# Two pairs per output group and 512-token feed-forward products in a fused SSD and bilinear FFN kernel

## The chip, the cores and the metric

The kernel runs on one core of a Trainium2 chip. The time is the device time of one execution in microseconds (us). The engines are named as in the profile: PE is TensorE, DVE is VectorE, ACT is ScalarE, POOL is GpSimd, and SP is SyncE, which here only issues DMAs.

## The reference

The input has 4 batches, 8 heads, 768 tokens, a head dimension of 32 and a state dimension of 16. A scan with decay runs along the tokens, then a feed-forward layer of 3072 tokens, 256 model and 1536 inner dimensions follows.

```python
log_a = np.log(np.clip(a, 1e-06, 1.0))
for c in range(nc):
    ...
    L = np.exp(cum[:, :, :, None] - cum[:, :, None, :]) * causal
    M = np.einsum('bhin,bhjn->bhij', Cc, Bc) * L
    y_intra = np.einsum('bhij,bhjd->bhid', M, xc)
    y_inter = np.einsum('bhin,bhnd->bhid', Cc, state) * decay_to_i[:, :, :, None]
    y[:, :, sl] = y_intra + y_inter
    Bx = np.einsum('bhjn,bhjd->bhjnd', Bc, xc) * decay_from_j[:, :, :, None, None]
    state = decay_full[:, :, None, None] * state + np.sum(Bx, axis=2)
...
x = attn_out.transpose(0, 2, 1, 3).reshape(B * S, H * D)
out = ((x @ w_a) * (x @ w_b)) @ w_out
```

## The kernel before

The tokens are cut into 6 blocks of 128. The four batches form two groups of two, so there are 12 pairs: pair p is block p // 2 and batches 2(p % 2) and 2(p % 2) + 1, which makes 256 tokens. One pair passes through these steps.

- Loads (`load1`, L126): B, C and x of a pair, two DMAs each, into buffers bn, cn and xn that exist three times. In the loop all of them go through SP's queue.
- Scaling on POOL: `scale_bc` (L251, L259) multiplies B and C by decay factors (fB, fC, which `fb` at L567 fills per block on DVE), `scale_x` (L245) makes x 16-bit. From pair 4 on, B is also copied into "planes" (L269), and `turn` (L308) lets SP issue a transposing DMA that makes the operands of the scores.
- Scores (L320): 32 small matmuls into four PSUM banks, SC0 and SC1 of two banks each. `mask` (L354) multiplies each bank by the causal mask on DVE and writes 16-bit T1; with `by_pool` ACT copies the bank first (L351) and POOL multiplies (L352).
- The output group: `outputs` (for pairs below 4, `pv`) puts into the same banks the state's part (L425, operand Sbd), the masked scores times x (`pv_u`, L363) and the sums of the next state (`ds_mm`, L380). ACT copies the outputs to X2T (L441 in three pieces). Then `state_sums` adds to the state on DVE (L468), and `state_spread` on POOL makes the next pair's Sbd and gU (L484, L491).
- The feed-forward product: one `unit(p, k2)` computes two of the 12 slices of the inner dimension for 256 tokens. `unit_mm` (L504) makes aps and bps, each four matmuls of 256 columns into one PSUM bank; ACT copies aps to asb (L518); DVE multiplies bps and asb to hk (L525). The four remaining PSUM banks (pool psf) go round among aps, bps and the output product ops in the order of allocation.
- The output product: `out_half` (L538) sums 12 matmuls of 256 columns over hk and Wo for 128 tokens, ACT scales (L553), SP stores (L555).

The order of the work is written out by hand (`manual_schedule`), and each engine takes its instructions in the order of the code. `unit` returns a function: PE's matmuls and ACT's copy stand where `unit` is called, DVE's product stands where the function is called. So masks and products can be put in any order on DVE. A prologue with warm-up matmuls covers pairs 0 to 2; a loop over p from 3 to 11 puts the scores and the group of pair p between the six units of pair p - 1 and the two output products of pair p - 2; a tail finishes pair 11.

In the loop before, the order on PE from pair 4 on is: scores, units 0 to 2, one output product, unit 3, the group, one output product, units 4 and 5. On DVE it is mask 0, product 0, masks 1 and 2, product 1, mask 3, products 2 and 3, the state sums, products 4 and 5.

Of the kernel before, what the change touches and what calls it, by code (L numbers as in the profile page):

```python
# [9 lines left out]
f32 = mybir.dt.float32  # L10
f16 = mybir.dt.float16
# [7 lines left out]
YS = 16.0  # L19
# [3 lines left out]
def kernel(  # L23
# [60 lines left out]
    X2T = big.tile([128, NP, 2, 2, Q], f16, name="X2T")  # L84
# [17 lines left out]
    mid = ctx.enter_context(tc.tile_pool(name="mid", bufs=3))  # L102
    ffh = ctx.enter_context(tc.tile_pool(name="ffh", bufs=4))
    ps4 = ctx.enter_context(tc.tile_pool(name="ps4", bufs=1, space=PSUM))
# [25 lines left out]

    def load(p, eng=None):
        tiles(p)
        return [load1(eng or nc.sync, p, w, bt) for w in range(3) for bt in range(2)]
# [284 lines left out]
    def outputs(p):  # L418
        s = st[p]
        SCt = (SC0, SC1)  # L420
        for m in range(4):
            for bt in range(2):
                rows = slice(32 * m, 32 * m + 32)
                half = 64 * ((m + bt) % 2)
                nc.tensor.matmul(  # L425
                    SCt[bt][half : half + 64, m // 2, 0:Q],
                    s["Sbd"][rows, bt],
                    s["CT"][rows, bt],
                    start=True,
                    stop=False,  # L430
                    skip_group_check=True,
                    tile_position=(32 * m, half),
                )
        py = {(bt, u): SCt[bt][:, u, 0:Q] for bt in range(2) for u in range(2)}
        for u in range(2):
            pv_u(p, u, py, False)
        if p // NBP < NBLK - 1:
            ds_mm(p, 256, [SC0[:, 1], SC1[:, 1]])
        whole, low, high = slice(0, 128), slice(0, 64), slice(64, 128)
        for bt, to, fr in ((0, whole, whole), (1, low, high), (1, high, low)):  # L440
            nc.scalar.activation(  # L441
                out=X2T[to, p, bt].rearrange("p u (i r) -> p u r i", r=2),
                in_=SCt[bt][fr, :, 0:Q].rearrange("p u (r i) -> p u r i", r=2),
                func=AF.Copy,
                scale=YS / XS,
            )
# [115 lines left out]

    def bank(name):
        return psf.tile([128, 512], f32, name=name, tag="ff")
# [81 lines left out]
    load_wo(1)  # L646
    x2 = [load1(nc.sync, 2, 2, bt) for bt in range(2)]
# [26 lines left out]
    load(3)  # L674
# [12 lines left out]
    load(4)  # L687
# [16 lines left out]
    for p in range(3, NP):  # L704
        scores(p)
        ri = p >= P0
        if p + 1 < NP:
            scale_bc(p + 1, 1, nc.gpsimd)
            scale_bc(p + 1, 0, nc.gpsimd)
            turn(p + 1)  # L710
        if (p - 1) // NBP < NBLK - 1:
            state_spread(p - 1)
        if p + 1 < NP:
            scale_x(p + 1, nc.gpsimd)
        if p + 2 < NP:
            load(p + 2)
        if p == 3:
            mask(product(p, 0))
            h()
            for m in range(1, 4):  # L720
                mask(product(p, m))
            out_half(1, 0)
            out_half(1, 1)
            go((2, 2))
        else:
            h = unit(p - 1, 0)
            mask(product(p, 0), ri=ri)
            h()
            mask(product(p, 1), ri=ri)
            mask(product(p, 2), ri=ri)  # L730
            h = unit(p - 1, 1)
            h()
            mask(product(p, 3), ri=ri)
            go((p - 1, 2))
            out_half(p - 2, 0)
            go((p - 1, 3))
        pull(p)
        outputs(p) if ri else pv(p)
        if p // NBP < NBLK - 1:
            state_sums(p)  # L740
        if p == 3:
            go((2, 3))
        else:
            out_half(p - 2, 1)
        if p % 2 == 0 and p // 2 + 1 < NBLK:
            fb(p // 2 + 1)
        go((p - 1, 4), (p - 1, 5))

    go((NP - 1, 0), (NP - 1, 1))
    out_half(NP - 2, 0)  # L750
    go((NP - 1, 2), (NP - 1, 3))
    out_half(NP - 2, 1)
    go((NP - 1, 4), (NP - 1, 5))
    out_half(NP - 1, 0)
    for part in range(2):
        o_ps = bank("ops")
        cols = slice(part * 128, part * 128 + 128)
        for k in range(NK):
            nc.tensor.matmul(  # L759
                o_ps[:, 0:128],  # L760
                st[NP - 1]["hk"][:, k, Q : 2 * Q],
                Wo[:, k, cols],
                start=(k == 0),
                stop=(k == NK - 1),
                skip_group_check=True,
            )
        o_sb = ffh.tile([128, d_model], f32, name="osb", tag="osb")
        if part == 0:
            nc.vector.tensor_scalar(o_sb[:, 0:128], o_ps[:, 0:128], 1.0 / (YS * YS), None, ALU.mult)
        else:  # L770
            nc.scalar.activation(out=o_sb[:, 0:128], in_=o_ps[:, 0:128], func=AF.Copy, scale=1.0 / (YS * YS))
        r0 = (2 * (NBP - 1) + 1) * S + (NBLK - 1) * Q
# [31 lines left out]
```

## Time and profile before

| Quantity | Value |
| --- | --- |
| Median of 3 runs | 127.15 us (127.08 to 128.66) |
| Profiled execution, its own time | 127.25 us |
| Its span, first to last instruction | 125.5 us |
| Granted TensorE clock | 1.000 |
| Busy: PE, DVE, ACT, POOL | 119.9, 88.8, 72.5, 56.6 us |
| PE weight loads (PEld), beside PE | 101.3 us |
| DMA | 13.79 MB, mean 110 GB/s |

The page shows one execution. Busy time is the sum of an engine's instructions. Matmuls are pipelined, so the time between the starts of two matmuls says more than the length of one. The chain of waits follows what ended last back through what released it; its pieces, in order of time, show where PE runs without a hole. In lines of groups, the numbers after the bar are the busy time in us, the mean in ns of one instruction, and the engine's idle time just before, with what ended it. In lines of the timeline, the first number is the start and the second the length, both in us. In lines of DMA issues, the last number is the median time in us from issue to landing.

### The profile page before, as it was taken

Reading aid. Unit: us, or ns where it says so; the run is one execution under the profiler, and the core shown is the slowest. Engines: PE = TensorE matmul, PEld = TensorE weight load, DVE = VectorE, ACT = ScalarE, POOL = GpSimd, SP = SyncE. Lnnn points to the kernel's source line nnn. Section 1 sums busy time; section 2 is a strip of 40 time slices with the busy share of each in tenths; the row PEclk is TensorE's granted clock in tenths of the full one; section 3 lists DMA queues with packets and bytes.
Section 4 is the critical chain, followed back from the end, with each engine's and each line's share of the span. In section 5 each row is a group of like instructions: output and inputs, shape, how many; then the busy total and the mean of one; then the engine's idle time right before and its main releaser. Section 6 shows DMA issues by size and latency. Waiting matters only on the chain.

```text
span 125.5 us, 4786 instructions
## 1 busy us (share of the span) xinstructions
PE 119.9 (96%) x1964; PEld 101.3 (81%) x1964; DVE 88.8 (71%) x165; ACT 72.5 (58%) x144; POOL 56.6 (45%) x100
## 2 busy tenths in 40 slices
PE   6979999999999999999999999999999999999990
PEld 2436789978898988888898898889889889899980
DVE  1588978894958958948959949959849739644440
ACT  0466666866365575575575475485485575674430
POOL 7999974957850933806508307508218000000000
PEclk9999999999999999999999999999999999999999
DMA  3999999974644666547646764454646210110112
GB/s 65 167 167 232 157 213 159 184 145 80 167 89 67 165 115 125 141 71 185 81 74 169 87 107 128 88 108 126 114 82 168 66 42 5 42 42 5 44 45 78
DMA packets 45493, 13.79 MB, mean 110 GB/s; under 512 B 40496, under 2 KB 45264, under 8 KB 45472
## 3 DMA queue, kind: packets, MB, share of 16 engines
q1 hardware_dynamic: 41520, 10.06, 38.4%
q0 software_dynamic: 1952, 3.08, 14.6%
q10 hardware_dynamic: 2000, 0.36, 1.6%
q8 instruction: 15, 0.25, 0.9%
q14 instruction: 6, 0.05, 0.1%
HBM read 11.13 MB, written 3.15 MB: 114 GB/s over the span
## 4 chain that ended last, share of the span: by engine, by line
PE 84%; DMA 6%; POOL 4%; DVE 2%; ACT 1%; issue 1%; ACTq 0%; POOLq 0%
PE aps L504 25%; PE bps L504 24%; PE ops L538 23%; DMA Wb<-in_moe_w_b_dram 6%; PE SC L320 3%; PE SC L363 3%; DVE t L354 2%; PE SC L380 1%; PE SC L425 1%; PE fps L221 1%; POOL cn L126 1%; PE ops L759 1%; POOL bn L126 1%; ACT bt L297 1%; POOL causal L181 1%
## 5 line engine op out<-in xcount | busy, mean ns | idle before, releaser
L525 DVE TENSOR_TENSOR hk<-bps,asb 128x512 f16<-128x512 f32 x72 | 49.1, 686 | 17.8 <-ACT asb L518 17.4
L518 ACT COPY asb<-aps 128x512 f32<-128x512 f32 x72 | 42.0, 586 | 17.4 <-PE aps L504 16.3
L504 PE MATMUL aps<-X2T,Wa 128*128 128x256 f16 x288 | 43.3, 273 | 0.0
L504 PE MATMUL bps<-X2T,Wb 128*128 128x256 f16 x288 | 42.9, 273 | 0.2 <-DMA Wb<-in_moe_w_b_dram 0.2
L538 PE MATMUL ops<-Wo,hk 128*128 128x256 f16 x276 | 33.9, 273 | 0.0
L504 PEld LDWEIGHTS <-Wb 128*128 128x128 f16 x288 | 29.6, 103 | 2.2 <-DMA Wb<-in_moe_w_b_dram 0.4
L504 PEld LDWEIGHTS <-Wa 128*128 128x128 f16 x288 | 28.5, 103 | 3.0 <-DMA Wa<-in_moe_w_a_dram 0.3
L538 PEld LDWEIGHTS <-hk 128*128 128x128 f16 x276 | 26.0, 98 | 3.6 <-DVE hk L525 0.2
L354 DVE TENSOR_TENSOR t<-SC,causal_ri 128x512 f16<-128x512 f32 x32 | 21.1, 680 | 0.0
L251 POOL TENSOR_TENSOR planes<-cn,fC 128x256 f16<-128x256 f32 x8 | 5.0, 621 | 33.7 <-DMA cn<-in_C_dram 23.1
L553 ACT ACTIVATE osb<-ops 128x256 f32<-128x256 f32 x23 | 8.8, 383 | 16.4 <-PE ops L538 16.2
L245 POOL TENSOR_SCALAR x<-xn 128x512 f16<-128x512 f32 x9 | 13.4, 1490 | 1.0 <-DMA xn<-in_x_dram 0.3
L441 ACT ACTIVATE X2T<-SC 64x256 f16<-64x256 f32 (+1 forms) x24 | 10.9, 456 | 4.9 <-PE SC L380 3.8
L468 DVE SCALAR_TENSOR_TENSOR U<-SC,G,gU 128x64 f32<-128x64 f32 x16 | 4.3, 282 | 7.0 <-ACT X2T L441 6.3
L354 DVE TENSOR_TENSOR t<-SC,causal 128x512 f16<-128x512 f32 x13 | 8.3, 682 | 0.9 <-PE SC L320 0.9
L259 POOL TENSOR_TENSOR bm<-bn,fB 128x256 f16<-128x256 f32 x11 | 7.0, 640 | 1.5 <-DMA bn<-in_B_dram 1.5
L193 PE MATMUL SC<-warm 128*128 128x512 f16 (+1 forms) x15 | 4.9, 474 | 1.2 <-DVE warm L162 1.2
L193 PEld LDWEIGHTS <-warm 128*128 128x128 f16 x22 | 2.3, 122 | 3.7 <-issue 1.9
L363 PEld LDWEIGHTS <-x 64*32 64x32 f16 x384 | 3.2, 91 | 2.2 <-ACT x L243 1.0
L363 PE MATMUL SC<-t,x 64*32 64x128 f16 x352 | 4.6, 219 | 0.0
L269 POOL COPY planes<-bm 128x128 f16<-128x128 f16 x16 | 4.2, 291 | 0.5
L352 POOL TENSOR_TENSOR t<-tmp,causal 128x512 f16<-128x512 f32 x3 | 3.5, 1156 | 1.3 <-DMA cn<-in_C_dram 1.0
(78 smaller groups left out, 81.0 us busy)
## 6 DMA issues: line engine op xcount, KB each, us to landing
out_dram<-osb SPq DMA_DIRECT2D x23, 128.0 KB, 2.5
xn<-in_x_dram SPq DMA_DIRECT2D x21, 128.0 KB, 3.8
bn<-in_B_dram SPq DMA_DIRECT2D x20, 64.0 KB, 3.0
cn<-in_C_dram SPq DMA_DIRECT2D x18, 64.0 KB, 3.1
Wa<-in_moe_w_a_dram POOLq DMA_DIRECT2D x2, 384.0 KB, 6.1
Wb<-in_moe_w_b_dram POOLq DMA_DIRECT2D x2, 384.0 KB, 7.5
Wo<-in_moe_w_out_dram POOLq DMA_DIRECT2D x2, 384.0 KB, 7.0
cn<-in_C_dram POOLq DMA_DIRECT2D x4, 64.0 KB, 5.2
```

What stands on the lines that cost most here:

```text
L193: nc.tensor.matmul(bank[:, 0:cols], warm[:, 0:128], warm[:, 0:cols], start=True, stop=True, skip_group_check=True)
L245: eng.tensor_scalar(xo, xi, XS, None, ALU.mult)
L251: eng.tensor_tensor(out=planes[p % 2][:, 4:6].rearrange("p r (h n) -> p r h n", n=N), in0=pair_in[p][which].rearrange("p h r n -> p r h n" ...
L259: eng.tensor_tensor(out=m_, in0=pair_in[p][which].rearrange("p h r n -> p r h n"), in1=(f[:, blk, :, bp] if factor is None else factor).un ...
L354: nc.vector.tensor_tensor(out=o_, in0=i_, in1=c_, op=ALU.mult)
L363: nc.tensor.matmul(py[bt, u][32 * (g ^ 2 * bt) : 32 * (g ^ 2 * bt) + 32] if p >= P0 else py[bt][32 * g : 32 * g + 32, u * Q : (u + 1) * Q] ...
L441: nc.scalar.activation(out=X2T[to, p, bt].rearrange("p u (i r) -> p u r i", r=2), in_=SCt[bt][fr, :, 0:Q].rearrange("p u (r i) -> p u r i" ...
L504: nc.tensor.matmul(ps[:, kk * 2 * Q : (kk + 1) * 2 * Q], W[k // 6][:, f, k % 6 // 3 * 384 : (k % 6 // 3 + 1) * 384].rearrange("p (c kk) -> ...
L518: (nc.vector.tensor_copy if on_dve else nc.scalar.copy)(asb, a_ps)
L525: nc.vector.tensor_tensor(out=s["hk"][:, 2 * k2 : 2 * k2 + 2, :].rearrange("p k q -> p (k q)"), in0=b_ps, in1=asb, op=ALU.mult)
L538: nc.tensor.matmul(o_ps[:, 0:d_model], hk[:, k, bt * Q : (bt + 1) * Q], Wo[:, k, :], start=(k == 0), stop=(k == NK - 1), skip_group_check= ...
L553: nc.scalar.activation(out=o_sb, in_=o_ps[:, 0:d_model], func=AF.Copy, scale=1.0 / (YS * YS))
```

## The change

From block 2 on, both pairs of a block share one output group. The outputs go to a new buffer XB, in which the 512 tokens of a block lie side by side with even and odd tokens in two halves; ACT no longer interleaves them when it copies. The feed-forward product is done for 512 tokens at once (`bunit`): aps and bps hold one of the 12 slices for 512 tokens, made by two matmuls of 512 columns each. `bout` makes the output product for a quarter of these tokens and stores it in two DMAs, one for even and one for odd rows.

The loads of B and C run one pair further ahead on SP, C before B. The loads of x are issued by POOL from pair 3 on. POOL scales x of pair p + 1 and B and C of pair p + 2 in the stage of pair p. The loop is replaced by an order written out stage by stage: `stage` issues the scores and what POOL, SP and the factors need, `masked` takes turns between masks and units, `group` does the shared output group and the state sums. Pairs 5 to 8 have one of their four masks on ACT and POOL. The pool mid has four buffers instead of three.

```diff
-    mid = ctx.enter_context(tc.tile_pool(name="mid", bufs=3))
+    mid = ctx.enter_context(tc.tile_pool(name="mid", bufs=4))
+    hkb = ctx.enter_context(tc.tile_pool(name="hkb", bufs=2))
...
-    def outputs(p):
+    def outputs(blk):
+        pairs = range(blk * NBP, (blk + 1) * NBP)
...
+        if blk < NBLK - 1:
+            for j, p in enumerate(pairs):
+                ds_mm(p, NBP * Q + 2 * D * j, [SC0[:, 1], SC1[:, 1]])
         whole, low, high = slice(0, 128), slice(0, 64), slice(64, 128)
         for bt, to, fr in ((0, whole, whole), (1, low, high), (1, high, low)):
             nc.scalar.activation(
-                out=X2T[to, p, bt].rearrange("p u (i r) -> p u r i", r=2),
-                in_=SCt[bt][fr, :, 0:Q].rearrange("p u (r i) -> p u r i", r=2),
+                out=XB[to, blk - P0 // NBP, :, bt].rearrange("p u j q -> p u (j q)"),
+                in_=SCt[bt][fr, :, 0 : NBP * Q],
...
+    def bunit(blk, k):
...
+        for W in (Wa, Wb):
+            t_ = psf.tile([128, 512], f32, name="aps" if W is Wa else "bps", tag="ff")
+            for f in range(2):
+                nc.tensor.matmul(
+                    t_,
...
+                    XB[:, blk - P0 // NBP, f].rearrange("p t j q -> p (t j q)"),
...
+        asb = evac_a(ps[0])
+        return lambda: nc.vector.tensor_tensor(out=s["hk"][:, k], in0=ps[1], in1=asb, op=ALU.mult)
...
+    def bout(blk, c, parts=1):
...
+        rows = out[(2 * j + bt) * S + blk * Q :][0:Q].rearrange("(i r) d -> r i d", r=2)
...
+            for r in range(2):
+                q = nc.scalar if parts > 1 and part and r else nc.sync
+                q.dma_start(rows[r, :, cs], o_sb[64 * r : 64 * r + 64, 0:w])
...
     load_wo(1)
+    tiles(3)
+    for bt in range(2):
+        load1(nc.gpsimd, 3, 2, bt)
...
-    load(3)
+    for bt in range(2):
+        load1(nc.sync, 3, 0, bt)
+    for bt in range(2):
+        load1(nc.sync, 3, 1, bt)
+    loads_bc(4)
+    loads_x(4)
...
+    def stage(p, by_pool, spread=()):
         scores(p)
...
+        if by_pool:
+            mask(product(p, 3), by_pool=True, ri=True)
+        if p % NBP == 0 and p // NBP + 1 < NBLK:
+            fb(p // NBP + 1)
+        loads_bc(p + 3)
+        prep_x(p + 1)
+        prep(p + 2, spread)
+        loads_x(p + 2)
+
+    def masked(p, ms, *units):
+        for i in range(max(len(ms), len(units))):
+            h = units[i]() if i < len(units) else None
+            if i < len(ms):
+                mask(product(p, ms[i]), ri=True)
+            if h:
+                h()
...
+    scores(4)
+    fb(3)
+    prep(5, (3,))
+    prep_x(5)
+    loads_x(6)
+    loads_bc(7)
+    prep(6)
+    masked(4, (0, 1))
+    out_half(2, 0)
+    masked(4, (2, 3), *pu(3, 0, 1, 2, 3))
+    stage(5, True)
+    masked(5, (0, 1))
+    out_half(2, 1)
+    masked(5, (2,), *pu(3, 4, 5))
+    group(2)
+    out_half(3, 0)
+    out_half(3, 1)
+
+    stage(6, True, (4, 5))
+    masked(6, (0, 1))
+    masked(6, (2,), *bu(2, 0, 1, 2, 3, 4))
+    stage(7, True)
+    masked(7, (0, 1, 2), *bu(2, 5, 6, 7, 8, 9, 10, 11))
+    group(3)
+    bout(2, 0)
+    bout(2, 1)
+
+    stage(8, True, (6, 7))
+    masked(8, (0, 1))
+    masked(8, (2,), *bu(3, 0, 1, 2, 3, 4, 5))
+    for blk in range(4, NBLK):
+        pB = blk * NBP + 1
+        stage(pB, False)
+        masked(pB, (0, 1))
+        bout(blk - 2, 2)
+        masked(pB, (2, 3), *bu(blk - 1, 6, 7, 8, 9))
+        group(blk)
+        bout(blk - 2, 3)
+        bgo(blk - 1, 10, 11)
+        if blk + 1 < NBLK:
+            stage(pB + 1, False, (pB - 1, pB))
+            masked(pB + 1, (0, 1))
+            bout(blk - 1, 0)
+            masked(pB + 1, (2,))
+            bout(blk - 1, 1)
+            masked(pB + 1, (3,), *bu(blk, 0, 1, 2, 3, 4, 5))
+    last = NBLK - 1
+    bout(last - 1, 0)
+    bout(last - 1, 1)
+    bgo(last, *range(6))
+    bout(last - 1, 2)
+    bgo(last, *range(6, NK))
+    bout(last - 1, 3)
+    for c in range(3):
+        bout(last, c)
+    bout(last, 3, 2)
```

In short: `prep(p)` is `scale_bc` for C and B and `turn`, followed by the state spreads that it is given; `prep_x(p)` is `scale_x`; `loads_bc` issues C and B on SP, `loads_x` issues x on POOL; `pu` and `bu` make lists of units of a pair or of a block; `bgo` runs units of a block with no mask between.

## The prediction

> **What bounds the kernel now.** I read the summary first, then the chain of waits in order of time, then the groups, the timeline around one unit, and the DMA issues.
>
> ```profile
> span 125.5 us, 4786 instructions
> ...
> PE 119.9 (96%) x1964; PEld 101.3 (81%) x1964; DVE 88.8 (71%) x165; ACT 72.5 (58%) x144; POOL 56.6 (45%) x100
> ...
> PE 84%; DMA 6%; POOL 4%; DVE 2%; ACT 1%; issue 1%; ACTq 0%; POOLq 0%
> ```
>
> The chain lies on PE for 84% of the span. Its pieces (start, length, engine, product, line) show whether PE has holes:
>
> ```profile
> 66.43 0.36 PE SC L320 x32
> ...
> 69.53 1.31 PE ops L538 x12
> 70.84 0.44 PE aps L504 x4
> 71.28 0.44 PE bps L504 x4
> ...
> 75.57 0.36 PE SC L320 x32
> ```
>
> From one pair's scores to the next is 75.57 - 66.43 = 9.14 us. In it lie 72 matmuls of 256 columns, 0.437/4 = 0.109 each, so 7.86; scores 0.36; the output group 0.70 (three steps, 0.19 + 0.25 + 0.26 between their starts); two entries of about 0.09 ahead of scores and group. That is 9.1: PE is full. Only fewer cycles on PE or new holes can move the time.
>
> The side engines:
>
> ```profile
> L525 DVE TENSOR_TENSOR hk<-bps,asb 128x512 f16<-128x512 f32 x72 | 49.1, 686 | 17.8 <-ACT asb L518 17.4
> L441 ACT ACTIVATE X2T<-SC 64x256 f16<-64x256 f32 x16 | 7.3, 454 | 0.3
> L416 ACT ACTIVATE X2T<-SC 128x512 f16<-128x512 f32 x2 | 1.2, 597 | 1.8 <-PE SC L363 1.2 <-PE SC L380 0.7
> L245 POOL TENSOR_SCALAR x<-xn 128x512 f16<-128x512 f32 x9 | 13.4, 1490 | 1.0 <-DMA xn<-in_x_dram 0.3
> ```
>
> ```profile
> 43.26 0.60 PE L504 MATMUL aps<-X2T,Wa 128*128 128x256 f16 x4
> ...
> 43.90 0.59 ACT L518 COPY asb<-aps 128x512 f32<-128x512 f32 x1
> ...
> 44.52 0.69 DVE L525 TENSOR_TENSOR hk<-bps,asb 128x512 f16<-128x512 f32 x1 [0.25 <-ACT asb L518]
> ...
> 50.33 1.28 DVE L354 TENSOR_TENSOR t<-SC,causal_ri 128x512 f16<-128x512 f32 x2
> ...
> 51.53 0.68 DVE L525 TENSOR_TENSOR hk<-bps,asb 128x512 f16<-128x512 f32 x1
> ```
>
> A unit that starts on PE at t has its copy at t+0.64 and its product at t+1.26, done at t+1.95. DVE operations queued back to back start 0.60 apart (51.53 - 50.33 for two). Products use four banks in turn, two per unit, so unit k+2's second half (bps) waits for the product of unit k. It wants its bank at t+2.16, two and a half units later: 0.2 of slack. In the loop of before, no burst of masks uses that up, because an output product (1.31) lies after the third unit.
>
> ```profile
> xn<-in_x_dram SPq DMA_DIRECT2D x21, 128.0 KB, 3.8
> ...
> cn<-in_C_dram POOLq DMA_DIRECT2D x4, 64.0 KB, 5.2
> xn<-in_x_dram POOLq DMA_DIRECT2D x2, 128.0 KB, 6.9
> ```
>
> **What the Trainium skill says.** "TensorE: Matmul & The Clock Gate", section "Back-to-back issue gap", prices a warm matmul at N/2.4 + 2.5 ns. For 256 columns this is 109.2, and the trace has 109; for 512 columns, which no product here shows back to back, it gives 215.8. "DMA: Bandwidth & Descriptors", section "Specifications", puts the first byte at about 1 us from GpSimd and 0.6 from SP and ACT. The trace agrees in direction: in the first 5 us C loads landed after 4.2 from GpSimd and 3.3 from ACT. The same page, section "Issuing engines are not separate DMA queues", says that all issuers share the same 16 DMA engines; up to 24 us the trace shows them busy throughout.
>
> **The change part by part**, in us, times on the trace of before.
>
> *Wider matmuls.* The first two products of a block (aps and bps) take 48 matmuls of 512 columns in place of 96 of 256: 48 x 215.8 = 10.36 against 96 x 109.2 = 10.48. Over blocks 2 to 5 that saves 0.12 x 4 = 0.5. PSUM tiles and the work of ACT and DVE per unit stay the same. Bounds: 0 to 0.6.
>
> *One group per block.* The same small matmuls in four groups instead of eight: four entries of 0.09 and a few 0.02 transitions less, 0.5 (0 to 0.8). PE alone therefore gains 1.0.
>
> *Evacuation.* Three ACT copies of 512 columns at 0.60, 1.8 in all, in place of 1.40 per pair. They start 0.25 after the group's end G. The state sums on DVE wait for them as before (0.28 each, 0.22 apart) and end at G+2.83. The next scores need these banks. Behind groups 2 and 3 stand two output products, 2.62 + 0.09 = 2.71, so scores wait 0.15 each: **0.3**. Behind group 4 stand one product and two units, 3.13: nothing. Cover gone, it would be up to 2.8.
>
> *The order of masks and products.* This is the main cost. Stage p is the code from the scores of pair p to the next scores; S is the start of scores, whose result reaches DVE at S+0.62 (scores at 25.29, mask at 25.91). Stages 6 and 8 queue three masks ahead of the first product, with five or six units back to back and no output product between. First unit at S+0.47; masks at S+0.62, 1.22, 1.82; first product at 2.42, done 3.11. The third unit's bps wants its bank at 2.63: 0.52 lost, twice: **1.04**. Stage 7 alternates mask and product, 1.20 per unit against 0.86 on PE: product 5 at S+1.85 (its copy waits on ACT until 1.24, behind the copy of scores for GpSimd), 6 at 3.05, 7 at 4.26, each done 0.69 later. Units 8 and 9 want banks at 3.49 and 4.64 and get them at 3.78 and 4.99, the first 0.29 shifting the second: **0.64**. Stage 4 has two masks ahead of the output product's end and two among the units; product 1 of pair 3 ends at 44.01, its bank is wanted at 43.86: 0.19 with the hand-over. Stages 9 and 11: last product of the earlier stage, three masks and two products; bank at S+4.97, wanted at 4.80: 0.17 each, **0.34**. Stages 5 and 10 have output products as cover: 0. Sum **2.2**. Bounds: 0, if the slack is larger than the trace shows, to 4, at 0.69 per DVE operation instead of 0.60.
>
> *x through GpSimd.* Two issues of 0.77 per pair go to GpSimd; SP loses two of 0.65. GpSimd's chain per pair: scaling x 1.49, B, C and their copies 1.76, state spreads 0.8, issues 1.54, then the landing of x before the next scaling; its mask (1.16) fits into that landing. I take a landing of 4.0 from issue: SP's 3.2 at 40 to 60 us plus GpSimd's 0.8. After the second issue 3.2 remain, so 8.8 per pair against 9.0 on PE. Walked from 37.2 (end of the issues for pair 5): B and C of 5 to 38.9, spread 39.7, x of 5 at 40.4 to 41.9, issues 43.4, pair 6 to 45.1, mask 5 to 47.1 (group 2 wants it at 48.2), x of 6 48.6, pair 7 50.3, issues 51.8, mask 6 (scores 52.4) to 54.9, x of 7 56.5, pair 8 58.2, spreads 59.8, issues 61.3, mask 7 to 62.5, which group 3 wants at 65.0. The next round ends its spreads at 77.2, wanted by group 4 at 81.0. So nothing, with 2.5 to spare. Queued behind a late x are B, C, the transposing DMA and, on SP, the stores behind that. Bounds: 0 to 4, below. The early x of pair 4 lies ahead of pair 2's mask on GpSimd (26.6 to 27.0): 0 to 0.1.
>
> *Loads earlier.* C of pair 3 is waited for at 28.89 on GpSimd, and PE's transposes follow at 30.21. x of pair 3, formerly issued at 24.92, behind it, now starts at 18.3 on DMA engines that are full. Its 1024 packets at 18.6 ns (38.4% of 16 x 125.5 us over 41520 packets) on 16 engines take 1.2. I take **0.5** (0 to 1.2). Earlier B and C free GpSimd from its 4.6 us waits per pair, which PE never felt: 0.
>
> *Stores in halves, tail.* SP per pair: before 6 x 0.65 + 1.25 + 2 x 0.52 = 6.2, after 4 x 0.65 + 1.25 + 4 x 0.52 = 5.9, beside 9 us of PE. At the end SP issues three quarters and ACT one; the third SP issue comes about when the last quarter is ready: 0 (-0.2 to 0.4). The hole of 0.15 ahead of the last pair's product goes, but four such stores remain covered.
>
> Sum: -1.0 + 0.3 + 2.2 + 0.5 = +2.0. The profiled execution took 127.25 (1.75 around its span), 0.1 over the median shown: 129.25, say **129.2**, +1.6%. About 2% is what a measurement of this kernel can tell from no change.
>
> **Rivals.** *GpSimd's ring sets the pace (slower).* For: two x loads from this queue took 6.9. Against: they met full DMA engines; SP's own x took 6.2 at 18 to 20 us and 3.2 later. It decides when a landing exceeds about 5.0. At 5.5, between both, the mask for group 3 ends at 66.5 (+1.4), the spreads for group 4 lose 1.8 more, group 5 0.4: +3.6, **132.8**. *Clean overlap.* DVE's bursts are absorbed and only PE's saving and the early load remain: -1.0 + 0.5, **126.7**. For: DVE is busy 71% only. Against: the 0.2 slack of the bank ring. *Faster by over 2%* needs 2.6 saved, and PE shows only 1.0.
>
> **Chances.** Forecast 0.52 (128.2 to 130.4), ring 0.22, clean overlap 0.20, more than one of the dear ends together 0.04, faster by over 2% 0.02. The line at +2% is 129.7; 0.15 of the forecast's part lies over it. So slower 0.15 + 0.22 + 0.04 = 0.41, faster 0.02, within 2% 0.57. The range 126.4 to 132.6 leaves out about 0.2.
>
> **What would show it.** Right: bps of 512 columns 0.43 per two matmuls; PE holes of about 0.5 before a bps in stages 6 and 8 and two in stage 7, released by hk on DVE; POOL's x waiting for DMA without PE waiting for it. Wrong: PE in the output group waiting for POOL (the ring); no holes (clean overlap); transposes of pair 3 later by over 1 us; GpSimd issues far from 0.77.

## The result, and the profile after

The changed kernel takes **132.57 us** (median of 4 runs, 131.91 to 133.58) against 127.21 us for the kernel before on the same chip. The ratio is 1.041, with a 95% interval of 1.031 to 1.051: slower by over 2%. Some executions of every kernel come out longer than its others, many of them at a lower granted clock, and the ratios here and below are of the shorter ones alone. The experiments ran on other chips of the kind, where the kernel before has medians of 127.1 to 127.9; each ratio is to the kernel before on the same chip.

The profiled execution took 133.21 us, its span is 131.5 us against 125.5. The likeliest case of the prediction gave 129.2. The time came out beside that of the ring rival (132.8), at the very end of the range that the prediction gave (126.4 to 132.6). As shown below, this is in part luck: the rival's late x is there, but PE feels it at another place, the cost that the forecast called the main one is all but absent, and one that it had put at nothing takes its room.

The summary and the chain of waits of the changed kernel, the lines that answer to the first ones shown of before:

```profile
span 131.5 us, 4400 instructions
...
PE 118.7 (90%) x1772; PEld 81.2 (62%) x1772; DVE 86.0 (65%) x161; ACT 70.8 (54%) x136; POOL 73.6 (56%) x122
...
DMA 37%; POOL 27%; PE 20%; issue 8%; SPq 1%; DVE 1%; ACT 1%; POOLq 0%; ACTq 0%
```

PE does less work (118.7 against 119.9 us), yet the chain has left it: 84% lay on PE before, 20% now, and 64% lie on transfers and POOL. The table of waits names the loop (us in total, times, longest):

```profile
POOL x L243 <- DMA xn<-in_x_dram: 18.0, 7, 3.8
...
PEld L318 <- DMA turned<-planes: 4.3, 3, 2.0
...
PE SC L318 <- DMA turned<-planes: 2.9, 3, 1.5
```

POOL waits 18 us for x. As such that costs nothing. But PE's scores wait three times for "turned", the output of the transposing DMA. Before, they never did. The timelines of POOL, SP and PE around pair 7 show how the two are tied:

```profile
52.44 1.42 POOL L128 DMA_DIRECT2D xn<-in_x_dram  x2
54.51 1.16 POOL L350 TENSOR_TENSOR t<-tmp,causal_ri 128x512 f16<-128x512 f32 x1 [0.66 <-ACT tmp L349]
59.12 1.49 POOL L243 TENSOR_SCALAR x<-xn 128x512 f16<-128x512 f32 x1 [3.45 <-DMA xn<-in_x_dram]
60.68 0.62 POOL L249 TENSOR_TENSOR planes<-cn,fC 128x256 f16<-128x256 f32 x1
```

```profile
52.92 1.27 SPq L306 DMA_TRANSPOSE turned<-planes  x1
...
62.50 1.24 SPq L306 DMA_TRANSPOSE turned<-planes  x1
```

```profile
57.60 0.59 PE L574 MATMUL bps<-XB,Wb 128*128 128x512 f16 x2
59.26 0.43 PE L318 MATMUL SC<-turned 32*64 32x128 f16 x32 [1.06 <-DMA turned<-planes]
...
77.26 0.43 PE L318 MATMUL SC<-turned 32*64 32x128 f16 x32 [1.49 <-DMA turned<-planes]
...
95.43 0.43 PE L318 MATMUL SC<-turned 32*64 32x128 f16 x32 [0.31 <-DMA turned<-planes]
```

x for pair 7 is asked for at 52.44, arrives at 59.1, and only then can POOL go on to the planes of pair 8. The transposing DMA for pair 7, issued at 52.92 right behind x, lands 6.2 later, as the end of PE's wait shows (the median before was 2.9); the one for pair 9 is issued late (72.57), because POOL has by then lost 3.45 and 2.74 waiting for x.

The end of the span, all stores (SPq is SP issuing DMAs; x11 in 8.12 us):

```profile
118.91 6.74 PE L601 MATMUL ops<-Wo,hkb 128*128 128x256 f16 x72
...
120.83 8.12 SPq L616 DMA_DIRECT2D out_dram<-osb  x11
...
125.87 0.28 ACT L613 ACTIVATE osb<-ops 128x128 f32<-128x128 f32 x1 [1.14 <-DMA out_dram<-osb]
126.18 0.58 ACTq L616 DMA_DIRECT2D out_dram<-osb  x1
```

PE ends at 125.65, SP issues stores until 128.95, the span ends at 131.5. The rows of DMA issues (KB each, median us to landing):

```profile
xn<-in_x_dram POOLq DMA_DIRECT2D x20, 128.0 KB, 4.2
out_dram<-osb SPq DMA_DIRECT2D x30, 64.0 KB, 2.1
```

Cutting both spans at four points puts every microsecond in a place. The third column is the first experiment below.

| Stretch, us | Before | After | x issued earlier |
| --- | --- | --- | --- |
| Start to first feed-forward matmul | 10.89 | 11.64 | 11.95 |
| To the scores of pair 3 | 20.64 | 21.26 | 20.64 |
| To the scores of pair 4 | 7.42 | 7.42 | 7.42 |
| To the end of the last matmul | 83.41 | 85.33 | 82.00 |
| To the end of the span | 3.14 | 5.85 | 6.19 |
| Sum | 125.5 | 131.5 | 128.2 |

So the +6.0 are: +0.75 ahead of the first matmul; +0.62 for the early loads; +1.92 in the middle; +2.71 at the end. The first is not put down to the change: this matmul waits for Wa, and the code up to there is the same in both kernels. It starts at 10.5 to 10.9 in the three profiles of the kernel before and its variants, and at 10.6 to 12.0 in the eleven of the changed kernel and its variants. Why it varies is not shown.

### The profile page after: what moved, and what is told of

The parts are those of the page before. It is cut to its first block, busy times and chain, and to the rows that moved or that the text cites. A ratio compares the mean times of both kernels' runs of the same rounds, so it can differ in the third digit from the quotient of the medians.

```text
span 131.5 us, 4400 instructions
## 1 busy us (share of the span) xinstructions
PE 118.7 (90%) x1772; PEld 81.2 (62%) x1772; DVE 86.0 (65%) x161; ACT 70.8 (54%) x136; POOL 73.6 (56%) x122
## 4 chain that ended last, share of the span: by engine, by line
DMA 37%; POOL 27%; PE 20%; issue 8%; SPq 1%; DVE 1%; ACT 1%; POOLq 0%; ACTq 0%
DMA xn<-in_x_dram 17%; DMA bn<-in_B_dram 10%; PE ops L601 7%; DMA turned<-planes 7%; PE bps L574 6%; PE aps L574 6%; POOL xn L128 4%; POOL bm L257 4%; POOL x L243 3%; DMA out_dram<-osb 2%; POOL planes L249 2%; POOL planes L267 2%; POOL sbd L479 2%; POOL gU L494 2%; POOL bn L128 1%
## 5 line engine op out<-in xcount | busy, mean ns | idle before, releaser
L586 DVE TENSOR_TENSOR hkb<-bps,asb 128x512 f16<-128x512 f32 x48 | 32.2, 688 | 13.5 <-ACT asb L521 12.8
L574 PE MATMUL aps<-XB,Wa 128*128 128x512 f16 x96 | 28.6, 379 | 0.0
L574 PE MATMUL bps<-XB,Wb 128*128 128x512 f16 x96 | 28.5, 379 | 0.0
L601 PE MATMUL ops<-Wo,hkb 128*128 128x256 f16 (+1 forms) x204 | 22.5, 267 | 0.0
L601 PEld LDWEIGHTS <-hkb 128*128 128x128 f16 x204 | 18.5, 98 | 3.0
L528 DVE TENSOR_TENSOR hk<-bps,asb 128x512 f16<-128x512 f32 x24 | 16.0, 683 | 3.3 <-ACT asb L521 2.8
L574 PEld LDWEIGHTS <-Wb 128*128 128x128 f16 x96 | 9.9, 103 | 10.9
L507 PE MATMUL aps<-X2T,Wa 128*128 128x256 f16 x96 | 14.3, 274 | 0.9 <-DMA Wa<-in_moe_w_a_dram 0.9
L507 PE MATMUL bps<-X2T,Wb 128*128 128x256 f16 x96 | 14.1, 273 | 0.3 <-DMA Wb<-in_moe_w_b_dram 0.3
L541 PE MATMUL ops<-Wo,hk 128*128 128x256 f16 x96 | 11.7, 273 | 0.1
L541 PEld LDWEIGHTS <-hk 128*128 128x128 f16 x96 | 8.8, 98 | 1.7 <-issue 0.4
```

The source lines that it names most:

```text
L507: nc.tensor.matmul(ps[:, kk * 2 * Q : (kk + 1) * 2 * Q], W[k // 6][:, f, k % 6 // 3 * 384 : (k % 6 // 3 + 1) * 384].rearrange("p (c kk) -> ...
L528: nc.vector.tensor_tensor(out=s["hk"][:, 2 * k2 : 2 * k2 + 2, :].rearrange("p k q -> p (k q)"), in0=b_ps, in1=asb, op=ALU.mult)
L541: nc.tensor.matmul(o_ps[:, 0:d_model], hk[:, k, bt * Q : (bt + 1) * Q], Wo[:, k, :], start=(k == 0), stop=(k == NK - 1), skip_group_check= ...
L574: nc.tensor.matmul(t_, W[k // 6][:, f, k % 6 // 3 * 384 : (k % 6 // 3 + 1) * 384].rearrange("p (c kk) -> p kk c", kk=3)[:, k % 3], XB[:, b ...
L586: return lambda: nc.vector.tensor_tensor(out=s["hk"][:, k], in0=ps[1], in1=asb, op=ALU.mult)
L601: nc.tensor.matmul(o_ps[:, 0:w], hk[:, k, c * Q : (c + 1) * Q], Wo[:, k, cs], start=(k == 0), stop=(k == NK - 1), skip_group_check=True,)
```

## The experiments

**1. Is it the place of x's issue, or its queue?** Theory: POOL waits for the landing of an x that it asked for just before; asked for one step earlier, ahead of the scaling of x, the landing is covered. Rivals: GpSimd's queue itself is slow, or the transposing DMA is slow by itself. Two kernels: the same early place with GpSimd, and with SP. Both do the whole work.

```diff
         loads_bc(p + 3)
+        loads_x(p + 2)
         prep_x(p + 1)
         prep(p + 2, spread)
-        loads_x(p + 2)
```

(likewise for the two stages written out; the second kernel also issues x on SP in place of GpSimd)

> The changed kernel with one thing moved: in each stage GpSimd issues x of pair p+2 before it scales x of pair p+1, not after the scaling of B and C. Theory 1 (GpSimd's ring: x lands late because it is issued last, and scaling, transposing DMA and scores queue behind it): GpSimd's waits for x fall from 18.0 us to under 5, PE's waits for the transposed operands at the scores of pairs 7, 9 and 11 (about 3.2 us together) fall under 1, and the time falls by 2 to 3 us, to 129 to 130. Rival (the transposing DMA itself lands late, 4.6 to 6.2 us after its issue in place of 2.9): the wait at pair 7 of 1.2 stays, the others shrink, and the time falls by 1 to 2 us.

> As the kernel with x issued first in each stage, but x goes through SP's queue, ahead of the transposing DMA. Theory 1 (only the place of the issue matters): within 0.7 us of the run with GpSimd as issuer, since 1.42 us per pair leave GpSimd, which then has time to spare. If the queue itself matters (first byte later from GpSimd): x lands after 3.2 in place of 3.8 to 4.6 us and this run is faster than that one by 0.5 to 1.5 us. If SP is the tight one (its stores are late already): slower than that run by 1 us or more.

With GpSimd: **129.95 us** (129.76 to 130.62), ratio 1.017 (1.011 to 1.023) to the kernel before, as expected. The chain of waits is back on PE, GpSimd's wait for x has left the table of waits, and the scores of pairs 7, 9 and 11 wait for nothing:

```profile
PE 80%; DMA 8%; ACT 3%; POOL 3%; issue 1%; SPq 0%; ACTq 0%; POOLq 0%
...
57.66 0.43 PE L318 MATMUL SC<-turned 32*64 32x128 f16 x32
...
74.00 0.43 PE L318 MATMUL SC<-turned 32*64 32x128 f16 x32
...
91.79 0.43 PE L318 MATMUL SC<-turned 32*64 32x128 f16 x32
```

From the scores of pair 4 to the last matmul it takes 82.00, 3.33 less than the changed kernel. The three waits account for 3.0 of that: the distance between scores shrinks by 1.06, 1.56 and 0.38. The transposing DMAs between 50 and 66 us land after 2.8 again, so they were not slow by themselves.

With SP: **133.56 us** (132.63 to 134.22), ratio 1.044 (1.036 to 1.052). GpSimd still waits 8.6 for x, in six pieces, but PE's waits at the scores of pairs 7, 9 and 11 are gone here as well. Two others come, in the prologue:

```profile
41.99 0.43 PE L318 MATMUL SC<-turned 32*64 32x128 f16 x32 [2.44 <-DMA turned<-planes]
49.52 0.43 PE L318 MATMUL SC<-turned 32*64 32x128 f16 x32 [0.53 <-DMA turned<-planes]
```

The first of them costs more than itself, because PE runs at about half its rate afterwards:

```profile
PEclk9999999999999599999999999999999999999998
...
42.35 2.71 PE L541 MATMUL ops<-Wo,hk 128*128 128x256 f16 x12
44.85 1.06 PE L507 MATMUL aps<-X2T,Wa 128*128 128x256 f16 x4
```

(PEclk is the granted TensorE clock in tenths, one digit for each fortieth of the span.) The twelve matmuls of the output product take 2.50, from their start to the next group's; in the kernel with GpSimd they take 1.32 (40.37 to 41.69). From the scores of pair 4 to those of pair 5 it is 7.53 in place of 5.27: 0.53 of waiting and some 1.7 of lower rate.

From the scores of pair 5 to those of pair 11 this kernel takes 96.21 - 49.52 = 46.7, the one with GpSimd 91.79 - 45.28 = 46.5. There the queue makes next to no difference; the place does. In the prologue SP's queue is the tight one, and its transposing DMA stands behind the x loads.

**2. What the queue costs in the kernel before.** If GpSimd's queue costs nothing, moving x to it in the old order should not be felt.

```diff
-        return [load1(eng or nc.sync, p, w, bt) for w in range(3) for bt in range(2)]
+        return [load1(nc.gpsimd if w == 2 else nc.sync, p, w, bt) for w in range(3) for bt in range(2)]
```

> The kernel before with one part of the change alone: in pairs 3 to 11 x is issued by GpSimd, at the same place in the code (after it has scaled x of the next pair). Theory 1 (late place on a queue that also has to consume x): x is wanted one stage later as before, GpSimd has 33 us of idle time, so the transposed operands come no later: within 0.8 us of the kernel before. Rival (GpSimd's queue itself is the loss): GpSimd waits for x and the scores or the group wait for it, 2 us or more slower.

**129.13 us** (128.47 to 130.98), ratio 1.013 (1.006 to 1.019). By the ratio that is 1.6 over the kernel before, twice the 0.8 expected. Two scores now wait, and one wait on GpSimd goes with them:

```profile
76.15 0.43 PE L320 MATMUL SC<-turned 32*64 32x128 f16 x32 [0.63 <-DMA turned<-planes]
...
86.53 0.43 PE L320 MATMUL SC<-turned 32*64 32x128 f16 x32 [1.17 <-DMA turned<-planes]
```

```profile
71.25 0.62 POOL L251 TENSOR_TENSOR planes<-cn,fC 128x256 f16<-128x256 f32 x1 [4.78 <-DMA cn<-in_C_dram]
```

On one queue, x had stood behind B and C, which are wanted first. From its own queue it starts beside them (issues at 65.05 and 65.36), and C, 5.2 from issue to use (its median landing before was 3.1), makes the planes late. This expectation was missed: it seems that the order within a queue had been doing a service. This is read from the trace; no run put that order back by itself.

**3. The end: row halves or bunched output products?** Five kernels bear on this. First all stores of the changed kernel are made whole, one DMA per tile with its rows interleaved by the access pattern. Beside it, only the last block's second halves go to GpSimd's queue.

```diff
-            for r in range(2):
-                q = nc.scalar if parts > 1 and part and r else nc.sync
-                q.dma_start(rows[r, :, cs], o_sb[64 * r : 64 * r + 64, 0:w])
+            q = nc.scalar if parts > 1 and part else nc.sync
+            q.dma_start(rows[:, :, cs], o_sb[:, 0:w])
```

```diff
-                q = nc.scalar if parts > 1 and part and r else nc.sync
+                q = nc.scalar if parts > 1 and part and r else nc.gpsimd if r and blk == NBLK - 1 else nc.sync
```

> The changed kernel with each output tile of the new output product stored by one DMA in place of two row halves; the rows in memory are the same. Theory 2 (SP's issue of 11 half stores, 0.47 to 1.6 us each, sets the end after PE is done): the stretch from PE's last matmul to the end of the span falls from 5.85 us to about 3.2, and the time by 2 to 3 us. Rival (the end is late because five output products now stand together at the end and each store is slow): the stretch stays above 5 and the time falls by less than 0.7.

> The changed kernel with the second row halves of the last block's stores issued by GpSimd, which has no other work left then. Theory 2 (SP's issue rate): the stretch from PE's last matmul to the end falls from 5.85 to 3.2 to 4, the time by 2 to 2.7 us. Rival (the DMA engines or the landing set the end): unchanged within 0.5 us.

The interleaved whole stores: **141.57 us** (139.66 to 143.26), ratio 1.098 (1.086 to 1.110). This told nothing on the question, but something else. The DMA row of its page (tenths, 40 slices) and two waits:

```profile
DMA  3999999976497665947806363061111110011110
```

```profile
DVE osb L611 <- DMA out_dram<-osb: 5.9, 1, 5.9
...
ACT osb L613 <- DMA out_dram<-osb: 3.8, 1, 3.8
```

In the last third, with little but stores, one to two tenths of the 16 DMA engines work, that is two or three. The Trainium skill, "DMA: Bandwidth & Descriptors", section "Why a DMA increments its semaphore by 16 and not by 1", says that the number of engines is the largest one up to 16 that divides the slowest dimension on both sides. Here that dimension is 2 on the DRAM side (even and odd rows), which gives two engines, and the row agrees.

The second halves on GpSimd: median 132.05 us (129.58 to 133.67), too spread for a ratio. In its profiled execution the end after the last matmul is 127.9 - 123.46 = 4.4 in place of 5.85: the issues on SP matter, though less than expected. Whether it is only that, and what is left, three kernels on top of experiment 1 show:

```diff
+    osp = ctx.enter_context(tc.tile_pool(name="osp", bufs=8))
...
-            o_sb = ffh.tile([128, d_model], f32, name="osb", tag="osb")
+            o_sb = osp.tile([128, d_model], f32, name="osb", tag="osb")
```

> The kernel with x issued first in each stage, and eight buffers in place of four for the output tiles of the new output product. In its predecessor the last ACT copy waited 1.49 us for an earlier store to land, and SP issued stores for 3.6 us after PE's last matmul. If the buffers set the end, the ACT copy follows PE by 0.1 us and the time falls by 1 to 1.5 us. If SP's issue rate sets it (11 half stores in 8.5 us), the ACT wait goes but the end does not move: within 0.4 us of 129.95.

> Both, and the second row halves of the last block's stores issued by GpSimd: SP's rate and the buffers are both taken away. Expected: the stretch from PE's last matmul to the end of the span 3.2 to 3.8 us as in the kernel before (3.1), where the predecessor has 6.2; the time 126.8 to 127.8, 0.3 to 1 us under the kernel before on the same chip, because PE's own work is 1.4 us shorter (110.1 against 111.5 us from the first product to the last). If clustering of five output products at the end costs by itself, it stays above 128.3.

Eight output buffers: **129.88 us** (129.24 to 130.15), ratio 1.021 (1.016 to 1.025). ACT's wait for a buffer is gone, and the end stays at 5.86. With the second halves on GpSimd too: **128.45 us** (127.91 to 129.05), ratio 1.011 (1.007 to 1.014), the end 4.4 and not the 3.2 to 3.8 expected. So it is not the buffer; SP has a part in it, which needs 0.47 to 0.71 for a half store (in the changed kernel and in that with eight buffers, one each took 1.5 to 1.6) and has eleven of them from the first output of the last row on. A second queue takes away half the surplus.

The other way round, halves in the kernel before, where output products are not bunched at the end:

```diff
-        (q or nc.sync).dma_start(out[r0 : r0 + Q, :], o_sb)
+        for r in range(2):
+            (q or nc.sync).dma_start(out[r0 + 64 * r : r0 + 64 * r + 64, :], o_sb[64 * r : 64 * r + 64, :])
```

> The kernel before with one part of the change alone: each output tile but the last is stored by two DMAs of 64 rows. SP has 6.2 us of issues per 9.1 us and gets 1.0 more. Theory 2 needs halves together with many output products at the end: here only three stand in the last 6 us, so within 0.6 us of the kernel before, at most 0.5 later at the end. Rival (halves cost by themselves): 1 us or more slower, with the transposing DMAs issued later on SP.

**128.51 us** (127.33 to 129.13, 12 runs), ratio 1.009 (1.005 to 1.013). Its end is 3.5 against 3.14. The runs fall into two groups. The profiled one belongs to the upper: it shows a granted clock of 0.6 to 0.7 in two early slices, ahead of the first store, and takes 22.24 from the first feed-forward matmul to the scores of pair 3 in place of 20.64. The lower group, five runs of 127.33 to 127.75, is some 0.4 over the kernel before, as its end is, and within the 0.6 expected. Seven of the twelve runs are in the upper group, but only 4 of 20 of the kernel before on that chip took over 128; whether the halves have to do with that is open.

**4. The early load of pair 3, and the search for a better version.** On top of the eight buffers, the loads of pairs 3 and 4 go back to where the kernel before has them, all on SP.

```diff
     load_wo(1)
-    tiles(3)
-    for bt in range(2):
-        load1(nc.gpsimd, 3, 2, bt)
...
-    for bt in range(2):
-        load1(nc.sync, 3, 0, bt)
-    for bt in range(2):
-        load1(nc.sync, 3, 1, bt)
-    loads_bc(4)
-    loads_x(4)
+    tiles(3)
+    for w in range(3):
+        for bt in range(2):
+            load1(nc.sync, 3, w, bt)
...
     scale(3)
+    tiles(4)
+    for w in range(3):
+        for bt in range(2):
+            load1(nc.sync, 4, w, bt)
     loads_bc(5)
```

> The kernel with x issued first in each stage and eight output buffers, and besides the loads of pairs 3 and 4 put back as in the kernel before: B, C and x of a pair in turn on SP, at their old places; B and C of pair 5 follow them. If the earlier x of pair 3 on full DMA engines is what makes PE's transposes of pair 3 wait for GpSimd (1.14 and 0.94 us in two of the profiles), the wait falls under 0.3, the scores of pair 3 start 20.6 us after the first product as before, and the time falls by 0.5 to 1.2 us from 129.88. Rival (chance of the DMA timing): the wait stays in place.

The median is 132.45 us (129.59 to 133.61), too spread for a ratio. The profiled execution (129.59) answers the question: from the first feed-forward matmul to the scores of pair 3 it takes 20.82, where the kernel with eight buffers needed 22.04 and its transposes waited 1.14 for the scaled B. But the scores of pair 4 now wait 1.39 for their transposing DMA, which stands on SP behind x of 4 and B and C of 5 and is issued at 35.65, 1.6 after its planes are ready. The gain is handed over to the next wait.

Two versions of this with another end: the last block's second halves on ACT's queue, or the last block's outputs interleaved again by ACT's copies, so that its tiles are stored whole.

```diff
-                q = nc.scalar if parts > 1 and part and r else nc.sync
+                q = nc.scalar if r and blk == NBLK - 1 else nc.sync
```

```diff
+            if blk == NBLK - 1:
+                for j in range(NBP):
+                    nc.scalar.activation(
+                        out=XB[to, blk - P0 // NBP, :, bt, j].rearrange("p u (i r) -> p u r i", r=2),
+                        in_=SCt[bt][fr, :, cols[j]].rearrange("p u (r i) -> p u r i", r=2),
...
+            if blk == NBLK - 1:
+                r0 = (2 * j + bt) * S + blk * Q
+                (nc.scalar if parts > 1 and part else nc.sync).dma_start(out[r0 : r0 + Q, cs], o_sb[:, 0:w])
+                continue
```

> The kernel with x first, old loads of pairs 3 and 4 and eight buffers; the second row halves of the last block go through ACT's queue. If two issuing queues are enough (half stores take 0.47 to 0.59 us each to issue), the stretch from PE's last matmul to the end falls from 5.8 to 3.3 to 3.8 us, below the 4.4 with GpSimd as second issuer; time 126.3 to 127.5. If ACT's copies are held up by its own issues: 4.4 or more.

> The same kernel, but in the last block ACT interleaves even and odd tokens again when it copies the group's outputs (six copies of 256 columns in place of three of 512), and each output tile is stored whole, by one DMA of contiguous rows. If the row halves are what makes the end late, the stretch from PE's last matmul to the end is 3.0 to 3.3 us as before (3.13), with 0 to 0.5 lost behind the slower copies: time 126.0 to 127.2, level with the kernel before or up to 1 us faster. If five output products at the end cost by themselves, the stretch stays above 4.

With ACT's queue the median is 128.98 us (126.38 to 133.25, 23 runs), with whole stores 128.80 (126.68 to 133.69, 22 runs); the kernel before has 127.16 on that chip. The ratios, 0.996 (0.990 to 1.002) from 3 of the 23 runs and 1.006 (1.004 to 1.009) from 11 of the 22, show neither version faster, and by the medians both are slower. The wait at the scores of pair 4 was 3.38 and 2.95 in the profiled executions, and PE ran at about half its rate after it here too: from there to the scores of pair 5 they took 6.94 and 6.93 in place of 5.27. The ends are clear: 4.05 with ACT's queue, between the two cases expected, and with whole stores

```profile
119.27 6.74 PE L611 MATMUL ops<-Wo,hkb 128*128 128x256 f16 x72
...
122.50 3.53 SPq L626 DMA_DIRECT2D out_dram<-osb  x4
...
126.35 0.38 ACTq L626 DMA_DIRECT2D out_dram<-osb  x1
```

the last matmul ends at 126.01 and the span at 129.2: 3.19, as before (3.14), with the same output products in one row at the end (x72 is four of twelve matmuls and a fifth in two halves of twelve each). So the row halves make the end late, not the bunching alone.

The last kernel puts the pieces together: x of pair 3 back on SP behind its B and C, x of pair 4 on GpSimd, eight buffers, whole stores in the last block.

> The kernel with x issued early by GpSimd and eight output buffers, with two more edits: x of pair 3 is loaded as in the kernel before (SP, behind B and C of pair 3) while x of pair 4 stays with GpSimd; and the last block's outputs are interleaved again by ACT, so that its output tiles are stored whole. Theory (the three costs of the change are the place of the x issue, the early load of x(3), and the stores in row halves at the end; its gain on PE is real): no wait for the transposing DMA at the scores of any pair, scores(3) 20.6 to 20.8 after the first feed-forward product, first to last matmul about 110.0 against 111.5 in the kernel before, 3.0 to 3.3 from the last matmul to the end; the time is 0 to 1 us under the kernel before, 126.0 to 127.2. Rival (SP's queue in the prologue cannot take x of pair 3 beside the earlier B and C without the first transposing DMA being late): the scores of pair 4 wait 0.5 or more for it, and the time is 127.5 to 129.

**127.66 us** (126.46 to 128.98, 22 runs), ratio 1.001 (0.999 to 1.004): level with the kernel before. The scores of pair 3 come 20.63 after the first feed-forward matmul and the end is 2.9, both as expected. But the rival was right on pair 4. From the timelines of PE, POOL and SP:

```profile
40.62 0.43 PE L319 MATMUL SC<-turned 32*64 32x128 f16 x32 [1.09 <-DMA turned<-planes]
```

```profile
31.84 1.50 POOL L244 TENSOR_SCALAR x<-xn 128x512 f16<-128x512 f32 x1 [2.50 <-DMA cn<-in_C_dram]
33.40 1.44 POOL L129 DMA_DIRECT2D xn<-in_x_dram  x2
```

```profile
36.67 1.32 SPq L307 DMA_TRANSPOSE turned<-planes  x1
```

x of pair 3, issued at 25.5, is scaled at 31.84 (the view names a DMA of C as the last to end the wait), behind it come the issue of x for pair 5 and the planes of pair 4; the transposing DMA is issued at 36.67 and lands 3.9 later. With the early load it had been issued at 36.29, and PE, having waited for pair 3, came at 40.16 and found it landed; now PE comes at 39.5. Taking the first wait away uncovers the second: of the 1.1 to 1.4 us gained up to the scores of pair 3, 1.1 are lost again. First to last matmul is 111.8; without this wait it would be 110.7 against 111.5. No version that beats the kernel before was found.

## Why the prediction was wrong, though its range held

The measured 132.57 lies inside the stated range by 0.03, and the ring rival's total is close to it. Both are luck: the sum of +2.0 was made of terms most of which were off, in both directions, and the rival's total holds the same 2.2 for the masks.

**The order of masks and products: 2.2 predicted, about 0.2 found.** This was "the main cost". The failed step is "products use four banks in turn, two per unit, so unit k+2's second half (bps) waits for the product of unit k". DVE's timeline of the changed kernel at the start of stage 6 and PE's third bps:

```profile
53.75 1.89 DVE L352 TENSOR_TENSOR t<-SC,causal_ri 128x512 f16<-128x512 f32 x3 [0.54 <-PE SC L318]
55.55 1.88 DVE L586 TENSOR_TENSOR hkb<-bps,asb 128x512 f16<-128x512 f32 x3
```

```profile
55.81 0.59 PE L574 MATMUL bps<-XB,Wb 128*128 128x512 f16 x2
```

Three masks stand ahead of the first product, as walked. That product runs from 55.55 to 56.24, and the third bps starts at 55.81, in the middle of it: it does not need the bank that this product frees. In the order of waits, the third bps waits for an ACT copy and the fourth unit's aps for the product: a bank freed by an earlier copy is given out first. By that order the slack is 0.64 (three units of 0.86, less the 1.95 after which a product is done) and not 0.2. In the kernel of experiment 1 the stretches from the scores of pairs 6, 7 and 8 to the next scores or group are 4.95, 6.67 and 5.74 long; the sums of their parts (0.43 per half unit, 0.36 for scores, 0.09 per entry) are 4.86, 6.59 and 5.72. Holes: 0.09, 0.08, 0.02, where 0.52, 0.64 and 0.52 were predicted. This is read from the traces; no kernel with another bank order was run.

**x through GpSimd: 0 predicted, 3.3 found.** The step that failed is the landing of 4.0, together with "8.8 per pair against 9.0 on PE". The landing's median is 4.2, but 5.5 for pair 7 and 4.6 for pair 8. And 9.0 is the step of the kernel before. In the new order more of PE's work stands behind the scores of pair 11: the stages of experiment 1 from pair 6 to pair 9 last 4.95, 10.6 and 5.74, so two pairs pass in 15.6 to 16.3, 7.8 to 8.2 each, which 8.8 doesn't fit even with 4.0. The ring rival had +3.6, near the 3.3 found, but its condition, a landing over 5.0, was met for pair 7 alone, and it expected PE to wait in the output group for masks and spreads. PE waited at the scores, since the planes and the transposing DMA stand behind x on POOL too. Pair 7 is a case by itself: its transposing DMA was issued in time and landed late, together with x, and why is not shown. The prediction had named this queue ("queued behind a late x are B, C, the transposing DMA") and not walked it.

**Stores and end: 0 predicted, 2.7 found.** The sentence "the third SP issue comes about when the last quarter is ready" counted quarters. SP has eleven half stores to issue from 120.83 on, and at the predicted 0.52 each it would have been busy until 126.6, after the last output is ready (126.15). At the measured mean of 0.74, short gaps and the one issue of 1.5 included, it was until 128.95. The 0.52 was that of a whole tile, and a half does not cost less (see the last section).

**PE's gain: 1.0 predicted, about 1.7 found.** The wider matmuls gave what was priced: eleven steps between starts, from 107.40 to 112.15 us, take 0.432 each (two matmuls of 512 columns) against 0.437, 0.5 over 96 of them, and 216 ns for one. The Trainium skill, "TensorE: Matmul & The Clock Gate", section "Back-to-back issue gap", gives 215.8 by the formula that the prediction used, but for an isolated matmul, and puts a sustained stream of this size at about 131 ns; the stream measured here shows 216. The shared group was under-priced: from its start to the next output product it takes 1.16 (79.23 to 80.39 in experiment 1) against two times 0.70, which with one entry less is 0.33 per block; with less for block 3 (1.20) and for the last block (0.92 against two times 0.54) it is 1.2 in all, not 0.5.

**Evacuation: 0.3 predicted.** In experiment 1 the scores of pair 6 follow 2.75 after the two output products behind group 2 start, their own length and the entry being 2.71. About 0.1 for the two groups.

**The early load: 0.5 predicted, 0.6 found.** In seven profiles with it, the scores of pair 3 come 20.6 to 22.0 after the first feed-forward matmul, mean 21.4; without it 20.5 to 20.8, but for the 22.24 at a lower clock in experiment 3. The size was right, with a wide spread, the place only in part. The prediction had PE's transposes of pair 3 wait behind C. They do so in four of the seven, by 0.68 to 1.14, but not in the profile of the changed kernel, where PE waits in the group of pair 2:

```profile
29.06 0.35 PE L361 MATMUL SC<-t,x 64*32 64x128 f16 x20 [0.21 <-ACT x L241]
...
29.72 0.29 PE L361 MATMUL SC<-t,x 64*32 64x128 f16 x12 [0.31 <-POOL t L350]
```

The first is x of pair 2, for whose landing ACT had waited 1.20; the second is GpSimd's mask, which starts at 28.50, right behind the issue of x of pair 4 (27.10), for which the prediction had 0 to 0.1.

Together: -1.7 + 0.2 + 0.1 + 3.3 + 0.6 + 2.7 = +5.2, with the 0.75 at the start about 6.0, as measured. The verdict "within 2%" rested on two errors that cancelled in part: a mechanism that was absent held the place of two that were there.

## What to carry to other kernels

Walk every queue that a moved step passes through to its last user, and compare it with the shortest stretch of work that must cover it, not with the mean of a block. A load that an engine asks for itself must stand ahead of the work that precedes its use on that engine, or its whole landing comes into that engine's chain. Where outputs leave in smaller pieces, count the issues left on the queue after the last matmul, at a cost measured for the smaller piece; and before pricing a bank conflict, read from the waits of the old kernel which instruction each bank's next user really waits for.

## What was not expected of the hardware

- A DMA can be outstanding while the engines stand nearly still. Between 55.6 and 57.2 us of the changed kernel, with x and the transposing DMA of pair 7 both issued over 1.4 us earlier and landed only at 59.1, the transfers of that window were

```profile
DMA packets 21, 0.01 MB, mean 8 GB/s; under 512 B 19, under 2 KB 19, under 8 KB 21
```

  What held them is not shown; full engines alone it was not.
- The same load from GpSimd landed after 2.9 to 5.9 us in the loop of the changed kernel, and the transposing DMA after 2.8 to 6.2.
- A store of half the rows costs SP more to issue than one of the whole tile (ns, least, median and most; L555 is whole tiles at the end of the kernel before, L616 the halves of the changed kernel):

```profile
L555 SPq DMA_DIRECT2D out_dram<-osb x5: 332/332/333, 107.7 to 121.5; - x5
...
L616 SPq DMA_DIRECT2D out_dram<-osb x33: 466/587/1619, 73.9 to 128.4; - x33
```

  All 23 whole tiles of the kernel before took 332 to 577, median 376; the halves of the kernel before in experiment 3 took 466 to 1042, median 588. So halves more than double the time that SP needs for a tile. Why is not shown.
- With stores whose slowest dimension is 2, the kernel is 9.8% slower than the kernel before, where the changed kernel is 4.1% slower; in its profile the end after the last matmul is 12.6 us long in place of 5.85.
- A long wait of PE cost more than itself. In four profiled executions PE waited 2.4 to 3.4 us at the scores of one pair (pair 4 in three of them, pair 9 with the interleaved stores), and each lost some 1.7 more to a lower granted clock right after it. After waits of 1.1 to 1.5 at the same places nothing more was lost. Where the limit lies is not shown, and in experiment 3 the clock fell once without such a wait.
